# Attention values and sums as matmuls of 64 columns: two banks for a pair of heads, each emptied by one instruction

## The chip, the core and the metric

The kernel runs on one core of a Trainium2 chip. Its engines run side by side: PE multiplies matrices into the banks of PSUM, DVE and ACT work element by element and are the two that empty banks, POOL works element by element on the rest of the memory, and SP issues the transfers. The metric is the device time of one execution in microseconds; lower is better. A "pass" below is one matmul record of the trace on PE: a float32 matmul leaves two records, each with its own load of weights, a float32r matmul leaves one.

## What is computed

```python
scores = scale * q @ k.T                    # 2 batches, 12 heads, 448 tokens, head size 64
scores = cap * tanh(scores / cap)
attn   = exp(scores - max); attn = attn / (sum(attn) + 1e-9)
x      = attn @ v                           # heads side by side: 896 tokens x 768
x      = moe(rms_norm(x) * g)               # gate and value 768 -> 1536, silu, 1536 -> 768
out    = ((x @ w1) * (x @ w2)) @ w3 @ w_out # 768 -> 1024 -> 1024 -> 768
```

Only the step `attn @ v` with its division by the sums is touched.

## The kernel before, in words

The heads are taken in 12 pairs. Scores lie transposed, 128 keys on the partitions by 448 queries, so a head of 448 keys has three chunks of 128 and one of 64. The last chunks of the two heads of a pair share one chunk, `c == 3`: head 0 in partitions 0 to 63, head 1 in 64 to 127. Two pairs are worked off in seven groups `g` of two banks; the fourth group holds the shared chunks of both pairs.

For each group PE makes the scores (`scores`, L430): six float32r matmuls over 64 rows each, which go in twos over the upper and the lower half of the array, or six over 128 rows for the fourth group. ACT takes them out with tanh (L438) and applies exp (L444). Then `pv` (L461) multiplies by the values. Before the change the stationary operand of a chunk is 128 columns wide, 64 of values and 64 of ones, so that one float32 matmul gives a head's values in partitions 0 to 63 of its bank and its sums in 64 to 127. A pair has two banks (tag `o`, two buffers), one for each head, started by its first chunk and stopped by its last; even pairs end with the shared chunk, odd pairs begin with it. Four instructions empty the two banks: `take_sum` twice (ACT L472 or DVE L474) and `take` twice (ACT L182 or DVE L184), 64 partitions each. The sums are inverted on DVE (L489), the values multiplied by them, and squares are summed for the norm. The next pair can only begin when both banks are empty.

Between these steps PE has other work that fills its waits: the first half of a product of the two last weight matrices (`item`, L640 to L642, 64 items of three matmuls over 384 columns), whose weights DVE, ACT and POOL prepare at the same time. Behind all of it, from L807 on, come the experts' products.

The order is not written by hand. A planner (`Plan`) is given every task with its engines and their costs, its rank and the buffers that it holds, plays the engines through by these costs and issues the tasks in the order in which they started there. Each engine then works its instructions off in that order. A grid below is the part of the array that a matmul takes: rows by columns, 128x128, 64x128, and in the changed kernel 128x64 and 64x64.

Of the kernel before, what the change touches and what calls it, by code (L numbers as in the profile page):

```python
# [10 lines left out]
F32 = mybir.dt.float32  # L11
# [3 lines left out]
AF = mybir.ActivationFunctionType  # L15
ALU = mybir.AluOpType
# [3 lines left out]
P = 128  # L20
B, H, S, D = 2, 12, 448, 64
BH = B * H
# [7 lines left out]
NK = 4  # L30
# [136 lines left out]
def body(ctx: ExitStack, tc, qk, v, cap, wgv, wdn, rg, w12, w3t, wo2, out):  # L167
    nc = tc.nc
# [43 lines left out]
    def layer(es, bounded):  # L212
# [12 lines left out]
        def ring(pool, tag, shape, dtype=F32, name=None):  # L225
            return pool.tile(shape, dtype, tag=tag, name=name or tag, bufs=rings[tag])
# [131 lines left out]
        def attend():  # L358
# [52 lines left out]
            def load_val(p):  # L411
                def run(e):
                    vals[p] = ring(ap, "v", [P, 7, P])
                    e.dma_start(out=vals[p], in_=v[p])

                v_done[p] = add(("SP", 0.45), run, first_of(p) - 5.5 if p else -6.85, makes=[vb[p]], size=P * 7 * P * 4)

# [30 lines left out]
            def pv(g, j):  # L448

                use = parts(g)  # L450
                p, c = use[j % len(use)]

                def run(e):
                    start = p % 2 == 0 and c == 0 or p % 2 == 1 and c == 3
                    stop = p % 2 == 0 and c == 3 or p % 2 == 1 and c == 2
                    for i in range(2):
                        rows = slice(i * D, (i + 1) * D) if c == 3 else slice(0, P)
                        if start:
                            pos[2 * p + i] = ring(ps, "o", [P, 512], name="po")
# [5 lines left out]
            def take_sum(i):  # L465
                def run(e):
                    pr, j = divmod(i, 2)
                    if j == 0:
                        sums[pr] = ring(ap, "sm", [P, S])
# [8 lines left out]
            def take(i):  # L478
                def run(e):
                    pr, j = divmod(i, 2)  # L480
                    b, h = divmod(pr, H // 2)
                    half(x_tile(b, h)[j * D : (j + 1) * D], pos[i][:D, :S], e)

                return run
# [39 lines left out]
            for g in range(NG):  # L524
# [12 lines left out]
                for j in range(len(use)):  # L537
# [12 lines left out]
                    r = g + 1.5  # L550
                    done = []
                    for i in range(2):
                        done.append(add(dict(ACT=0.66, DVE=0.66), take_sum(2 * p + i), r - 2 + i * 0.01, after=[a] + done[:1],
                                        makes=[] if i else [smb[p]], uses=[both[i]] + ([smb[p]] if i else [])))
                        new = b not in x_alloc
                        x = add(dict(ACT=0.57, DVE=0.66), take(2 * p + i), r - 2 + 0.1 + i * 0.01, after=[a] + ([] if new else [x_alloc[b]]),
                                makes=[xb[b]] if new else [], uses=[both[i]] + ([] if new else [xb[b]]))
                        x_alloc.setdefault(b, x)
                        done.append(x)
                    inv = [add(("DVE", 1.52), invert(p, c), r + 0.1 * c, after=done, uses=[smb[p]]) for c in range(2)]  # L560
# [101 lines left out]
        def attend_any():  # L662
# [4 lines left out]
            for i in range(BH):  # L667
# [3 lines left out]
                nc.sync.dma_start(out=t, in_=qk[pr])  # L671
                tv = pool.tile([P, 7, P], F32, tag="v", name="tv")
                nc.sync.dma_start(out=tv, in_=v[pr])
# [28 lines left out]
                for k in range(NK):  # L702
                    nc.tensor.matmul(po, tv[:, order[k], :D], pt[:, k, :], start=(k == 0), stop=(k == NK - 1))
                x = x_tile(b, h)
# [418 lines left out]
def _layout(a):  # L1123
# [6 lines left out]
    qk = np.concatenate([q, np.concatenate([one, two], axis=1)], axis=2)  # L1130
    v = np.concatenate([a["v"].reshape(BH, S, D), np.ones((BH, S, D), np.float32)], axis=2).reshape(BH // 2, 2, S, P)
    both = np.concatenate([v[:, 0, 3 * P :], v[:, 1, :D]], axis=1)[:, None]
    v = np.stack([v[:, 0, : 3 * P].reshape(-1, 3, P, P), v[:, 1, D:].reshape(-1, 3, P, P)], axis=2).reshape(-1, 6, P, P)
    v = np.concatenate([v, both], axis=1).transpose(0, 2, 1, 3)
# [31 lines left out]
```

## Time and profile before

| | |
|---|---|
| median of 3 runs | 636.42 us (636.06 to 638.11) |
| the profiled execution | 638.36 us, its span 636.6 us |
| PE busy | 619.9 us (97%) |
| DVE, ACT, POOL busy | 427.2, 284.4, 158.0 us |
| granted clock of PE, mean | 0.995 |

The span is the time from the first to the last instruction of the trace; 1.76 us of the profiled execution lie around it. PE's busy time is no measure of how full it is, since matmuls are pipelined and a record also counts the time in which it waits for the one ahead of it. The distance between the starts of neighbouring records tells more, and is used below.

### The profile page before, as it was taken

Reading aid. Unit: us, or ns where it says so; the run is one execution under the profiler, and the core shown is the slowest. Engines: PE = TensorE matmul, PEld = TensorE weight load, DVE = VectorE, ACT = ScalarE, POOL = GpSimd, SP = SyncE. Lnnn points to the kernel's source line nnn. Section 1 sums busy time; section 2 is a strip of 40 time slices with the busy share of each in tenths; the row PEclk is TensorE's granted clock in tenths of the full one; section 3 lists DMA queues with packets and bytes.
Section 4 is the critical chain, followed back from the end, with each engine's and each line's share of the span. In section 5 each row is a group of like instructions: output and inputs, shape, how many; then the busy total and the mean of one; then the engine's idle time right before and its main releaser. Section 6 shows DMA issues by size and latency. Waiting matters only on the chain.

```text
span 636.6 us, 7787 instructions
## 1 busy us (share of the span) xinstructions
PE 619.9 (97%) x2949; PEld 522.0 (82%) x2949; DVE 427.2 (67%) x543; ACT 284.4 (45%) x392; POOL 158.0 (25%) x153
## 2 busy tenths in 40 slices
PE   6999999999999999999999999999999999999996
PEld 2455556669999999999999999999999999999995
DVE  2898999979867677534777555566656765636743
ACT  6798788965533333322234222344323343313220
POOL 1747532213122344411132222211122121000000
PEclk9899999999999999999999999999999999999998
DMA  8554542325445346224993333323222324105111
GB/s 310 175 198 141 196 142 69 126 74 186 139 146 160 131 133 230 92 67 159 295 315 101 103 118 124 102 100 99 100 99 100 111 89 133 33 1 148 44 59 63
DMA packets 29758, 82.91 MB, mean 130 GB/s; under 512 B 2960, under 2 KB 16912, under 8 KB 29712
## 3 DMA queue, kind: packets, MB, share of 16 engines
q1 hardware_dynamic: 29712, 82.33, 38.9%
q8 instruction: 25, 0.41, 0.3%
q14 instruction: 21, 0.17, 0.1%
HBM read 73.27 MB, written 9.04 MB: 129 GB/s over the span
## 4 chain that ended last, share of the span: by engine, by line
PE 84%; DVE 7%; ACT 5%; issue 2%; POOL 1%; DMA 1%; SPq 0%; DVEq 0%; POOLq 0%
PE bank L808 22%; PE bank L809 22%; PE bank L807 22%; PE bank L1031 8%; PE po L461 4%; ACT t L438 2%; DVE sm L489 2%; PE pss L430 2%; ACT t L444 2%; PE bank L640 1%; PE bank L641 1%; PE bank L642 1%; DVE wraw L270 1%; DVE wraw L274 1%; POOL xraw L497 1%
## 5 line engine op out<-in xcount | busy, mean ns | idle before, releaser
L189 DVE TENSOR_TENSOR whl<-wraw,whl 128x768 fp32r<-128x768 f32 (+1 forms) x86 | 75.7, 882 | 70.4 <-POOL whl L186 58.2
L266 POOL TENSOR_SCALAR wraw<-wraw 128x768 int32<-128x768 uint32 (+1 forms) x67 | 76.1, 1135 | 170.8 <-DMA wraw<-in_w 57.8
L809 PE MATMUL bank<-xn,whl 128*128 128x448 f32 x288 | 106.0, 368 | 0.0
L808 PE MATMUL bank<-xn,whl 128*128 128x448 f32 x288 | 106.0, 368 | 0.0
L807 PE MATMUL bank<-xn,whl 128*128 128x448 f32 x288 | 106.0, 368 | 0.0
L270 DVE SCALAR_TENSOR_TENSOR wraw<-wraw 128x768 int32<-128x768 int32 (+1 forms) x76 | 71.4, 939 | 40.8 <-POOL wraw L266 33.6
L461 PE MATMUL po<-t,v 128*128 128x448 f32 (+1 forms) x192 | 75.5, 565 | 2.8 <-DVE xraw L184 1.2
L274 DVE SCALAR_TENSOR_TENSOR wraw<-wraw 128x768 int32<-128x768 int32 (+1 forms) x76 | 76.8, 1011 | 1.5
L186 POOL TENSOR_SCALAR whl<-wraw 128x768 fp32r<-128x768 f32 (+1 forms) x38 | 34.0, 895 | 166.8 <-PE bank L809 125.2
L809 PE MATMUL bank<-y,whl 128*128 128x448 f32 x192 | 70.7, 368 | 0.0
L807 PE MATMUL bank<-y,whl 128*128 128x448 f32 x192 | 70.7, 368 | 0.0
L808 PE MATMUL bank<-y,whl 128*128 128x448 f32 x192 | 70.7, 368 | 0.0
L182 ACT ACTIVATE whl<-wraw 128x768 fp32r<-128x768 f32 (+1 forms) x48 | 38.1, 795 | 70.6 <-PE bank L809 31.5
L257 ACT ACTIVATE wraw<-wraw 128x768 f32<-128x768 f32 (+1 forms) x55 | 48.5, 882 | 39.4 <-DMA wraw<-in_wgv 14.3
L461 PEld LDWEIGHTS po<-t,v 128*128 128x128 f32 (+1 forms) x192 | 31.5, 192 | 33.8 <-issue 25.9
L808 PEld LDWEIGHTS bank<-xn,whl 128*128 128x128 f32 x288 | 54.1, 188 | 5.5
L807 PEld LDWEIGHTS bank<-xn,whl 128*128 128x128 f32 x288 | 54.1, 188 | 5.4
L809 PEld LDWEIGHTS bank<-xn,whl 128*128 128x128 f32 x288 | 54.1, 188 | 5.4
L809 PE MATMUL bank<-u,whl 128*128 128x448 f32 x144 | 53.0, 368 | 0.0
L807 PE MATMUL bank<-u,whl 128*128 128x448 f32 x144 | 53.0, 368 | 0.0
L808 PE MATMUL bank<-u,whl 128*128 128x448 f32 x144 | 53.0, 368 | 0.0
L438 ACT ACTIVATE t<-pss,small 128x896 f32<-128x896 f32 x42 | 41.9, 998 | 10.3 <-PE pss L430 8.5
(103 smaller groups left out, 1007.5 us busy)
## 6 DMA issues: line engine op xcount, KB each, us to landing
wraw<-in_wgv SPq DMA_DIRECT2D x24, 768.0 KB, 4.4
wraw<-in_w SPq DMA_DIRECT2D x16, 768.0 KB, 4.2
wraw<-in_wdn SPq DMA_DIRECT2D x12, 768.0 KB, 4.2
wraw<-in_w3t SPq DMA_DIRECT2D x16, 512.0 KB, 4.0
wraw<-in_wo SPq DMA_DIRECT2D x8, 768.0 KB, 6.5
v<-in_v SPq DMA_DIRECT2D x12, 448.0 KB, 4.0
qk<-in_qk SPq DMA_DIRECT2D x11, 480.0 KB, 4.1
m_half<-mo SPq DMA_DIRECT2D x16, 192.0 KB, 1.9
```

The lines of the kernel that those rows point to most:

```text
L182: nc.scalar.activation(out_, in_, AF.Copy)
L189: e.tensor_tensor(lo, raw, r32(hi), op=ALU.subtract)
L257: e.activation(h, h, AF.Copy, scale=2.0**-112)
L266: e.tensor_scalar(l, l.bitcast(U32), 0.876 * 2.0**-29, 0.49, op0=ALU.mult, op1=ALU.add)
L270: e.scalar_tensor_tensor(l, h, 3, l, op0=ALU.logical_shift_left, op1=ALU.bitwise_or)
L274: e.scalar_tensor_tensor(l, h, -(2**31), l, op0=ALU.bitwise_and, op1=ALU.bitwise_or)
L438: e.activation(chunks[g], s[:, :, :S], AF.Tanh, scale=tsc)
L461: e.matmul(pos[2 * p + i][:, :S], vals[p][rows, 6 if c == 3 else 2 * c + i, :], x, start=start, stop=stop)
L807: e.matmul(dst, whi[:, c, :], src(0, g, b), start=(g == 0), stop=False)
L808: e.matmul(dst, whi[:, c, :], src(1, g, b), start=False, stop=False)
L809: e.matmul(dst, wlo[:, c, :], src(0, g, b), start=False, stop=(g == total - 1))
L1031: e.matmul(st["bank", name], w[:, q, :], z_at(op, q, y), start=q == 0 and n == 0, stop=q == NQ - 1 and n == 2)
```

## The change

The values lose their columns of ones: `v` is loaded as 7 x 64 columns instead of 7 x 128, and the ones come from the constant tile `ones`. A pair's two banks are divided otherwise: `po` holds the values of both heads, head 0 in partitions 0 to 63 and head 1 in 64 to 127, and `pn` their sums in the same places. Each chunk now takes four float32 matmuls over 64 columns instead of two over 128: values of head 0 and head 1, which take the left and the right half of the array's columns, then sums of head 0 and head 1. For the shared chunk each of them takes 64 rows by 64 columns. One `take_sum` and one `take` over 128 partitions empty the two banks.

```diff
@@ load_val
-                    vals[p] = ring(ap, "v", [P, 7, P])
+                    vals[p] = ring(ap, "v", [P, 7, D])
@@ pv
-                    for i in range(2):
-                        rows = slice(i * D, (i + 1) * D) if c == 3 else slice(0, P)
-                        if start:
-                            pos[2 * p + i] = ring(ps, "o", [P, 512], name="po")
-                        x = chunks[g][rows, j if c == 3 else i, :]
-                        e.matmul(pos[2 * p + i][:, :S], vals[p][rows, 6 if c == 3 else 2 * c + i, :], x, start=start, stop=stop)
+                    if start:
+                        pos[p] = [ring(ps, "o", [P, 512], name=name) for name in ("po", "pn")]
+                    for n in range(2):
+                        for i in range(2):
+                            to = slice(i * D, (i + 1) * D)
+                            rows = to if c == 3 else slice(0, P)
+                            x = chunks[g][rows, j if c == 3 else i, :]
+                            w = ones[rows, :D] if n else vals[p][rows, 6 if c == 3 else 2 * c + i, :]
+                            e.matmul(pos[p][n][to, :S], w, x, start=start, stop=stop)
@@ take_sum, take
-                    s = slice(j * D, (j + 1) * D)
                     if e is nc.scalar:
-                        e.activation(sums[pr][s], pos[i][D:, :S], AF.Identity, bias=guard[D:])
+                        e.activation(sums[pr], pos[pr][1][:, :S], AF.Identity, bias=guard)
                     else:
-                        e.tensor_scalar(sums[pr][s], pos[i][D:, :S], guard[D:], None, op0=ALU.add)
+                        e.tensor_scalar(sums[pr], pos[pr][1][:, :S], guard, None, op0=ALU.add)
...
-                    half(x_tile(b, h)[j * D : (j + 1) * D], pos[i][:D, :S], e)
+                    half(x_tile(*divmod(pr, H // 2)), pos[pr][0][:, :S], e)
@@ the planner's tasks
-                        ("PE", 1.65 if c < 3 else 0.97), pv(g, j), g + 1 + 0.1 * j, after=[exps[g], v_done[p], pv_last.get(p)],
+                        ("PE", 1.65), pv(g, j), g + 1 + 0.1 * j, after=[exps[g], v_done[p], pv_last.get(p)],
...
-                    for i in range(2):
-                        done.append(add(dict(ACT=0.66, DVE=0.66), take_sum(2 * p + i), r - 2 + i * 0.01, after=[a] + done[:1],
...
-                        x = add(dict(ACT=0.57, DVE=0.66), take(2 * p + i), r - 2 + 0.1 + i * 0.01, after=[a] + ([] if new else [x_alloc[b]]),
...
+                    done = [add(dict(ACT=0.55, DVE=0.64), take_sum(p), r - 2, after=[a], makes=[smb[p]], uses=[both[1]])]
+                    done.append(add(dict(ACT=0.55, DVE=0.64), take(p), r - 1.9, after=[a] + ([] if new else [x_alloc[b]]),
```

The planner makes another order of the new tasks. The first place is PE, from the last chunk of the third pair (the shared chunk) to the first chunks of the fourth; the names are `pss` the scores' banks, `t` the exp'd scores, `bank<-wo,whl` the filling items. Before:

```order
L461 MATMUL po<-t,v 128x448 x2
L430 MATMUL pss<-th 128x448 x6
L640 MATMUL bank<-wo,whl 128x384
L641 MATMUL bank<-wo,whl 128x384
L642 MATMUL bank<-wo,whl 128x384
L430 MATMUL pss<-th 128x448 x6
L640 MATMUL bank<-wo,whl 128x384
L641 MATMUL bank<-wo,whl 128x384
L642 MATMUL bank<-wo,whl 128x384
...
L461 MATMUL po<-t,v 128x448 x6
```

The same place of the changed kernel:

```order
L464 MATMUL po<-t,v 64x448 x2
L464 MATMUL pn<-t,ones 64x448 x2
L430 MATMUL pss<-th 128x448 x12
L634 MATMUL bank<-wo,whl 128x384
L635 MATMUL bank<-wo,whl 128x384
L636 MATMUL bank<-wo,whl 128x384
L464 MATMUL po<-t,v 64x448 x2
L464 MATMUL pn<-t,ones 64x448 x2
L464 MATMUL po<-t,v 64x448 x2
L464 MATMUL pn<-t,ones 64x448 x2
```

Between the end of one pair and the start of the next there stood two groups of scores and three filling items, and now there stand two groups and one item. Over the whole stage 33 of the 64 items stood ahead of the last `pv`, and now 15 do. Counted in program order up to the first expert matmul, neighbouring matmuls differ in their grid 61 times before and 78 times now; 12 of the 78 are between 64x128 and 128x128, and 36 lead into a grid of 64 columns.

The second place is DVE, from the emptying of the third pair's banks to that of the fourth pair's (`sm` the sums, `xraw` the values). Before:

```order
L184 COPY xraw<-po 64x448
L474 TENSOR_SCALAR sm<-po,small 64x448
L489 RECIPROCAL sm<-sm 128x224 x2
L189 TENSOR_TENSOR th<-qk,th 128x960
L270 SCALAR_TENSOR_TENSOR wraw<-wraw 128x768
L515 TENSOR_TENSOR acc<-acc,sq 128x448
L474 TENSOR_SCALAR sm<-po,small 64x448
L184 COPY xraw<-po 64x448
L474 TENSOR_SCALAR sm<-po,small 64x448
L489 RECIPROCAL sm<-sm 128x224 x2
```

The changed kernel:

```order
L474 TENSOR_SCALAR sm<-pn,small 128x448
L184 COPY xraw<-po 128x448
L487 RECIPROCAL sm<-sm 128x224 x2
L189 TENSOR_TENSOR th<-qk,th 128x960
L189 TENSOR_TENSOR wo<-wraw,wo 128x768 x2
L513 TENSOR_TENSOR acc<-acc,sq 128x448
L474 TENSOR_SCALAR sm<-pn,small 128x448
L487 RECIPROCAL sm<-sm 128x224 x2
```

Of the 48 instructions that emptied banks DVE had 22 and ACT 26; of the 24 now, DVE has 13 and ACT 11.

## Rows read from the trace of the kernel before

**Rows 1.** Busy time by stretch: length, PE, PEld, DVE, ACT, POOL, clock, DMA share, GB/s.

```profile
60.70:83.00 22.30, 21.02 (x92) 11.84 (x90) 22.10 (x23) 18.10 (x23) 13.40 (x13) 1.00 0.49 157
...
158.20:625.00 466.80, 466.80 (x2292) 427.06 (x2291) 291.67 (x390) 158.56 (x238) 95.83 (x89) 1.00 0.37 121
```

**Rows 2.** PE's groups, 0 to 158 us: count | busy us, mean ns | idle, releasers.

```profile
L461 PE MATMUL po<-t,v 128*128 128x448 f32 x144 | 61.7, 565 | 1.7 <-ACT t L444 0.8 <-ACT xraw L182 0.6 <-DVE xraw L184 0.4
L430 PE MATMUL pss<-th 64*128 64x448 f32 x198 | 29.9, 408 | 1.2 <-ACT t L438 1.2
L640 PE MATMUL bank<-wo,whl 128*128 128x384 f32 x64 | 23.6, 369 | 0.4 <-DVE mo L184 0.4
...
L461 PE MATMUL po<-t,v 64*128 64x448 f32 x48 | 14.2, 567 | 1.1 <-DVE xraw L184 0.8 <-ACT xraw L182 0.3
L430 PE MATMUL pss<-th 128*128 128x448 f32 x33 | 8.8, 400 | 0.0
L430 PE MATMUL pss<-qk 64*128 64x448 f32 x12 | 4.3, 873 | 5.0 <-DMA qk<-in_qk 5.0
L305 PE MATMUL bank<-acc,ones 128*128 128x448 f32 x4 | 1.8, 537 | 0.0
```

**Rows 3.** PE in order of time (start, length): first matmul, an item, first expert.

```profile
5.01 4.28 PE L430 MATMUL pss<-qk 64*128 64x448 f32 x12 [5.01 <-DMA qk<-in_qk]
...
157.21 0.33 PE L640 MATMUL bank<-wo,whl 128*128 128x384 f32 x1
...
158.25 0.36 PE L807 MATMUL bank<-xn,whl 128*128 128x448 f32 x1
```

**Rows 4.** PE in order of time, changes of grid, 37 to 42 us.

```profile
37.10 0.87 PE L430 MATMUL pss<-th 64*128 64x448 f32 x6
37.90 1.77 PE L461 MATMUL po<-t,v 128*128 128x448 f32 x4
39.60 0.86 PE L430 MATMUL pss<-th 64*128 64x448 f32 x6
40.30 0.91 PE L461 MATMUL po<-t,v 64*128 64x448 f32 x4
...
41.74 0.45 PE L640 MATMUL bank<-wo,whl 128*128 128x384 f32 x1
```

**Rows 5.** PE's weight loads in order of time; five neighbours, first and last.

```profile
46.35 0.19 PEld L461 LDWEIGHTS po<-t,v 128*128 128x128 f32 x1 [0.19 <-issue]
...
47.85 0.19 PEld L461 LDWEIGHTS po<-t,v 128*128 128x128 f32 x1 [0.18 <-issue]
```

**Rows 6.** PE in order of time where a pair waits for its banks, 20 to 34 us.

```profile
20.35 1.02 PE L461 MATMUL po<-t,v 64*128 64x448 f32 x2 [0.81 <-DVE xraw L184]
21.64 5.87 PE L461 MATMUL po<-t,v 64*128 64x448 f32 x10 [0.27 <-ACT xraw L182]
27.44 1.50 PE L430 MATMUL pss<-th 64*128 64x448 f32 x12
28.87 1.77 PE L461 MATMUL po<-t,v 128*128 128x448 f32 x4
...
32.01 1.02 PE L461 MATMUL po<-t,v 128*128 128x448 f32 x2 [0.58 <-ACT xraw L182]
33.41 1.02 PE L461 MATMUL po<-t,v 128*128 128x448 f32 x2 [0.37 <-DVE xraw L184]
```

**Rows 7.** Busy time and granted clock (third last column) behind such a wait.

```profile
22.20:25.65 3.45, 3.45 (x6) 1.51 (x5) 3.45 (x3) 3.29 (x4) 0.66 (x1) 0.51 0.31 108
```

**Rows 8.** Groups of instructions that empty the pairs' banks, 0 to 158 us.

```profile
L472 ACT ACTIVATE sm<-po,small 64x448 f32<-64x448 f32 x13 | 8.2, 631 | 0.8 <-PE po L461 0.4
L182 ACT ACTIVATE xraw<-po 64x448 f32<-64x448 f32 x13 | 7.0, 537 | 2.6 <-DVE sm L474 2.4
...
L184 DVE COPY xraw<-po 64x448 f32<-64x448 f32 x11 | 6.8, 616 | 2.3 <-ACT sm L472 2.1
```

**Rows 9.** The page's transfers: KB each, microseconds to landing.

```profile
v<-in_v SPq DMA_DIRECT2D x12, 448.0 KB, 4.0
```

More of the change, by code (lines that the diff above doesn't have):

```diff
@@ L412, in run @@
                 def run(e):
-                    vals[p] = ring(ap, "v", [P, 7, P])
+                    vals[p] = ring(ap, "v", [P, 7, D])
                     e.dma_start(out=vals[p], in_=v[p])
-                v_done[p] = add(("SP", 0.45), run, first_of(p) - 5.5 if p else -6.85, makes=[vb[p]], size=P * 7 * P * 4)
+                v_done[p] = add(("SP", 0.45), run, first_of(p) - 5.5 if p else -6.85, makes=[vb[p]], size=P * 7 * D * 4)
             def scores(g):
@@ L455, in run, with take_sum, take @@
                     stop = p % 2 == 0 and c == 3 or p % 2 == 1 and c == 2
[L456 to L461 removed]
+                    if start:
[7 more added lines that the diff above has]
+                            e.matmul(pos[p][n][to, :S], w, x, start=start, stop=stop)
                 return run
[L465 removed]
+            def take_sum(pr):
                 def run(e):
[L467 to L470 removed]
+                    sums[pr] = ring(ap, "sm", [P, S])
                     if e is nc.scalar:
[L472 removed]
+                        e.activation(sums[pr], pos[pr][1][:, :S], AF.Identity, bias=guard)
                     else:
[L474 removed]
+                        e.tensor_scalar(sums[pr], pos[pr][1][:, :S], guard, None, op0=ALU.add)
                 return run
[L478 removed]
+            def take(pr):
                 def run(e):
[L480 to L482 removed]
+                    half(x_tile(*divmod(pr, H // 2)), pos[pr][0][:, :S], e)
                 return run
@@ L550, in attend @@
                     r = g + 1.5
-                    done = []
-                    for i in range(2):
-                        done.append(add(dict(ACT=0.66, DVE=0.66), take_sum(2 * p + i), r - 2 + i * 0.01, after=[a] + done[:1],
-                                        makes=[] if i else [smb[p]], uses=[both[i]] + ([smb[p]] if i else [])))
-                        new = b not in x_alloc
-                        x = add(dict(ACT=0.57, DVE=0.66), take(2 * p + i), r - 2 + 0.1 + i * 0.01, after=[a] + ([] if new else [x_alloc[b]]),
-                                makes=[xb[b]] if new else [], uses=[both[i]] + ([] if new else [xb[b]]))
-                        x_alloc.setdefault(b, x)
-                        done.append(x)
+                    new = b not in x_alloc
+                    done = [add(dict(ACT=0.55, DVE=0.64), take_sum(p), r - 2, after=[a], makes=[smb[p]], uses=[both[1]])]
+                    done.append(add(dict(ACT=0.55, DVE=0.64), take(p), r - 1.9, after=[a] + ([] if new else [x_alloc[b]]),
+                                    makes=[xb[b]] if new else [], uses=[both[0]] + ([] if new else [xb[b]])))
+                    x_alloc.setdefault(b, done[1])
                     inv = [add(("DVE", 1.52), invert(p, c), r + 0.1 * c, after=done, uses=[smb[p]]) for c in range(2)]
@@ L671, in attend_any @@
                 nc.sync.dma_start(out=t, in_=qk[pr])
[L672 removed]
+                tv = pool.tile([P, 7, D], F32, tag="v", name="tv")
                 nc.sync.dma_start(out=tv, in_=v[pr])
@@ L702, in attend_any @@
                 for k in range(NK):
-                    nc.tensor.matmul(po, tv[:, order[k], :D], pt[:, k, :], start=(k == 0), stop=(k == NK - 1))
+                    nc.tensor.matmul(po, tv[:, order[k], :], pt[:, k, :], start=(k == 0), stop=(k == NK - 1))
                 x = x_tile(b, h)
@@ L1130, in _layout @@
     qk = np.concatenate([q, np.concatenate([one, two], axis=1)], axis=2)
-    v = np.concatenate([a["v"].reshape(BH, S, D), np.ones((BH, S, D), np.float32)], axis=2).reshape(BH // 2, 2, S, P)
+    v = a["v"].reshape(BH // 2, 2, S, D)
     both = np.concatenate([v[:, 0, 3 * P :], v[:, 1, :D]], axis=1)[:, None]
-    v = np.stack([v[:, 0, : 3 * P].reshape(-1, 3, P, P), v[:, 1, D:].reshape(-1, 3, P, P)], axis=2).reshape(-1, 6, P, P)
+    v = np.stack([v[:, 0, : 3 * P].reshape(-1, 3, P, D), v[:, 1, D:].reshape(-1, 3, P, D)], axis=2).reshape(-1, 6, P, D)
     v = np.concatenate([v, both], axis=1).transpose(0, 2, 1, 3)
```

## The prediction

> **What bounds the kernel now.** I read the busy time by stretch first, then PE's groups, then PE in order of time. From 158 us to 625 us PE is busy for the whole stretch at full clock [rows 1]: behind the first expert matmul it waits for nothing, so what the change does ahead of that point moves the end by as much. Ahead of it DVE is nearly as full as PE in places (22.10 of 22.30 us, [rows 1]), and the question is which of the two sets the pace.
>
> So I draw up an account of PE from its first matmul, 5.01 us, to the first expert matmul, 158.25 us [rows 3]: 153.2 us. The price of each kind of work is the distance between starts where PE runs without a break:
>
> - A float32 pass over 448 columns: from the first to the last of five weight loads 1.50 us [rows 5], so 0.375. The 144 passes over 128x128 [rows 2] take 54.0.
> - The 48 passes over 64 rows [rows 2] go in twos: four of them start at 40.30, six passes of scores follow, and the item behind these starts 1.44 us later [rows 4]. That is two slots of 0.375, the scores and little more. So 24 slots, 9.0.
> - Six passes of scores over 64 rows: twelve take 1.43 (27.44 to 28.87, [rows 6]), six 0.80 (37.10 to 37.90, [rows 4]); the difference, 0.63, is the work of six. 198 of them [rows 2] are 33 times 0.63, 20.8. The 33 over 128 rows at a third of that, 0.21 each, are 6.9.
> - A filling item: two take 1.04 (157.21 to 158.25, [rows 3]), so 64 items [rows 2] take 33.3.
> - The first pair's scores, 12 float32 passes in twos, 2.3, and four passes of `L305`, 1.5 [rows 2].
>
> Together 127.8. What is over from the six passes, 0.80 - 0.63 = 0.17, and from `pv` between scores, 37.90 to 39.60 = 1.70 less four passes, 0.20 [rows 4], is what PE loses when the grid changes: part of it before the change (the matmuls ahead run out), part behind it (a load of weights that nothing covers). The scores at 39.60 have only the part behind, since the shared chunk that follows has their grid: 0.70 - 0.63 = 0.07 [rows 4]. I take 0.19 for one change; 61 of them are 11.6. The rest, 153.2 - 139.4 = 13.8 us, are waits and slow clock. So PE's work with its grid changes is 91% of the stage, and DVE's load, however full, can only show in the 13.8.
>
> Of these, the waits for the pairs' banks are seen best at 20 to 34 us. At 20.35 the second pair's first `pv` has waited 0.81 us for DVE's copy, and its other half for ACT's until 21.64 [rows 6]. From 20.35 to 27.44 PE does four half passes (two slots) and eight full ones, 3.75, and one change and a half of grid, 0.3; it takes 7.09. The other 3.0 are the halves going one after the other, the second wait, and the clock: behind the gap the granted clock is 0.51 of full speed for 3.45 us [rows 7], which is the lower level, 1.2 GHz. At 32.01 and 33.41 the third pair waits again, 0.58 us and then some 0.6 between the two starts that are not work [rows 6]. That makes 0.8 + 3.0 + 0.6 + 0.6 = 5.0 us behind banks that four instructions empty, two on each bank, 0.54 to 0.63 us apiece [rows 8].
>
> **The change part by part.**
>
> *PE, chunks of 128 keys.* 72 matmuls over 128 columns become 144 over 64. If left and right half of the columns run side by side, as upper and lower half of the rows do [rows 4], a chunk takes four slots as before: nothing.
>
> *PE, the shared chunk.* Two matmuls, two slots side by side, become four, four slots: values and sums no longer come out of one matmul, and there is no other half of the array to give the sums to. 12 chunks x 2 slots x 0.375 = **+9.0 us**. Nothing hides it, since PE sets the pace.
>
> *PE, changes of grid.* 78 for 61: `pv` shares its grid with nothing now, neither with the filling items nor, for the shared chunk, with the scores. 17 x 0.19 = **+3.2 us**. No row shows a grid of 64 columns. From below, the part behind the change could vanish with the shorter load of weights; from above it is the 0.19 of any other change. The part behind the change is about half of it (0.07 of 0.17 above), and I estimate that half as many columns take half as long to load: 36 entries x 0.04 = **-1.4 us**; the ends are -3.4 (36 x 0.095) and 0.
>
> The Trainium skill (TensorE: Matmul & The Clock Gate, LDWEIGHTS) gives a load as columns over 1.2 GHz, so 53 ns less for 64 columns than for 128. By that the 36 entries would give back an estimated 1.9 us in place of 1.4; no run here shows it yet.
>
> *Emptying the banks.* 24 instructions for 48, over 128 partitions for 64. Nothing shows one over 128 partitions out of these banks; I take the 0.54 to 0.63 us of the old ones [rows 8], since they have as many elements in each partition. From above, at twice that, nothing is won. One instruction on each of ACT and DVE empties both banks at once, and the order has two groups of scores and an item to cover it, 2 x 0.63 + 0.52 and two changes, some 2.1 us. I let the whole 5.0 go: **-5.0 us**; the ends are 0, and with the other waits that the freed 14 us of ACT and DVE could shorten, some -10 (3 of the 13.8 are the start, where the first scores wait for ACT and run at low clock).
>
> *Order and transfers.* 18 items move behind the last `pv`: they are paid there instead, at the same price, and give DVE longer to finish the second batch's norm before the experts need it: nothing. The values' transfers halve, from 448 KB in 4.0 us [rows 9]; the scores, tanh and exp that lie ahead of a `pv` hide them, and none of PE's groups names them as a releaser [rows 2]: nothing; uncovered, 4.0 us for the first.
>
> Sum: 9.0 + 3.2 - 1.4 - 5.0 = **+5.8 us**. The profiled execution took 638.36 us (span 636.6 and 1.76 around it), so 644.2 against it; the median of the three runs is 1.9 lower, and against that I forecast **642.2 us**. With all waits kept it is +10.8, 647.2; with the best ends (-3.4 and -10) -1.2, 635.2.
>
> **The rivals.**
>
> *The waits vanish altogether, no change.* Those of 20 to 34 us are not the only ones: a DVE freed of 9 instructions and an ACT freed of 15 could give up the others. For it: DVE is 99% busy in one stretch [rows 1]. Against: the freed time matters only at the gaps. 9.0 + 3.2 - 1.4 - 10 = +0.8, 637.2.
>
> *The shared chunk's halves do not run together.* Before, they wrote to two banks; now both write to one, in different partitions and from different rows. If one waits for the other, each of the 12 chunks takes eight slots in place of four: 12 x 4 x 0.375 = +18, 660.2. No row shows two halves of the rows at work in one bank. The Trainium skill (TensorEngine Tiling, Gotcha 1: PSUM Pressure) says that different row tiles cannot access the same PSUM bank at once; by that this rival is the forecast. I hold it down because the two meet in no partition.
>
> *Halves of the columns do not run together.* Both read all 128 partitions, while the halves of rows that the trace shows read their own. If they go one after the other, each of 36 chunks takes eight slots: 36 x 1.5 = +54, and the shared ones +18 as well; the remaining waits, some 8, would drown in it: 642.2 + 72 - 8, about 706. For it: nothing in the trace has two matmuls reading the same partitions. Against: a float32r pass takes 0.21 us for the same columns [rows 4, 6], so a float32 pass asks for little more than half of what the array can be fed.
>
> *Changes to and from a grid of 64 columns are free, faster.* Then only the 12 between 64x128 and 128x128 are paid, 2.3 for 11.6: 9.0 - 9.3 - 5.0 = -5.3, 631.1. It decides if a change with such a grid costs under about 0.08 us (9.0 + 2.3 + 66 x price = 11.6 + 5.0). For it: no such grid was seen. Against: both directions between the grids that are seen cost about the same [rows 4].
>
> **How the numbers follow.** Forecast with its own range of 638.5 to 647.2: 0.62. Waits vanish: 0.13. Shared halves apart: 0.08. Column halves apart: 0.08. Free changes: 0.09. A measurement of this kernel can tell 0.3%, 1.9 us, from no change: faster is below 634.5, slower above 638.3. Faster: free changes and a sliver of the vanished waits, 0.10. Same: the rest of these, 0.13. Slower: 0.77. The range leaves out free changes and column halves apart, 0.17: from 636 to 661.
>
> **What would show it.** Starts of `pv` passes in twos a few ns apart with 0.375 us between twos say that column halves run together; four slots for the shared chunk, that its halves do. Scores between two `pv` at 0.80 and a lone `pv` at 1.65 to 1.70 say that the changes of grid are priced rightly. No gap at the second pair's start and a granted clock of 1.00 behind 20 us say that the 5.0 were won. The account up to the first expert matmul should come to about 159 us, with eight to nine of waits in it, and PE should be busy throughout behind it. The forecast is wrong if the waits only move: if with 15 items in place of 33 PE runs out of filling work and stands in front of tanh or exp, or if the experts find their weights late.

## The result and the profile after

The changed kernel takes 641.78 us (641.05 to 643.49); the kernel before, on the same chip, 637.46 us (635.54 to 640.34). The ratio is 1.0067, with an interval of 1.0048 to 1.0086: 4.3 us slower, where 5.8 were forecast. The profiled execution took 643.46 us, span 641.7.

Busy time by stretch of the changed kernel, with the columns of [rows 1] and the stretch of [rows 7]; PE's groups up to the first expert matmul, with the columns of [rows 2], follow it:

```profile
20.00:80.00 60.00, 56.31 (x310) 23.88 (x310) 59.43 (x57) 49.18 (x58) 33.77 (x31) 1.00 0.50 159
22.20:25.65 3.45, 3.45 (x22) 1.11 (x16) 3.45 (x3) 1.93 (x3) 2.35 (x3) 1.00 0.40 140
60.70:83.00 22.30, 22.30 (x129) 9.89 (x129) 21.76 (x27) 19.18 (x23) 8.57 (x10) 1.00 0.46 141
165.03:625.00 459.97, 459.97 (x2270) 423.24 (x2270) 287.71 (x383) 158.67 (x239) 97.93 (x92) 1.00 0.37 124
```

The first of these stretches in the kernel before, and below it the one group of [rows 2] that waited there and is not among them:

```profile
20.00:80.00 60.00, 57.14 (x228) 31.01 (x230) 57.39 (x56) 50.68 (x60) 34.96 (x31) 0.97 0.53 176
```

```profile
L641 PE MATMUL bank<-wo,whl 128*128 128x384 f32 x64 | 21.6, 338 | 1.3 <-DVE wo L189 1.3
```

PE's groups of the changed kernel:

```profile
L464 PE MATMUL po<-t,v 128*64 128x448 f32 x144 | 34.4, 556 | 0.6 <-DVE sm L474 0.5
L464 PE MATMUL pn<-t,ones 128*64 128x448 f32 x144 | 33.2, 539 | 0.0
L430 PE MATMUL pss<-th 64*128 64x448 f32 x198 | 28.0, 392 | 0.4 <-ACT t L438 0.4
L634 PE MATMUL bank<-wo,whl 128*128 128x384 f32 x64 | 22.7, 354 | 2.8 <-ACT mo L182 2.7
...
L464 PE MATMUL po<-t,v 64*64 64x448 f32 x48 | 11.6, 562 | 2.8 <-DVE xraw L184 1.5 <-DVE sm L474 1.3
L464 PE MATMUL pn<-t,ones 64*64 64x448 f32 x48 | 11.0, 536 | 0.0
...
L430 PE MATMUL pss<-qk 128*128 128x448 f32 x2 | 1.0, 591 | 0.3 <-ACT t L438 0.3
```

The granted clock is 1.00 where [rows 7] had 0.51, and the 12 transfers of the values land in 3.5 us for the 4.0 of [rows 9]. Behind the first expert matmul PE is busy throughout, as before. In front of it the waits have other places: behind the emptying of the banks 3.3 us (1.5, 1.3 and 0.5), where [rows 6] has 2.0, and at the filling items 2.8, nearly all behind ACT's `mo` copies, where the kernel before had 1.7 (0.4 and 1.3). PE in order of time (start, length) shows these, and the slots:

```profile
16.80 0.86 PE L430 MATMUL pss<-th 64*128 64x448 f32 x6
17.59 0.97 PE L464 MATMUL po<-t,v 64*64 64x448 f32 x4
18.39 0.92 PE L464 MATMUL pn<-t,ones 64*64 64x448 f32 x4
19.24 0.87 PE L430 MATMUL pss<-th 64*128 64x448 f32 x6
21.62 0.97 PE L464 MATMUL po<-t,v 64*64 64x448 f32 x4 [1.51 <-DVE xraw L184]
...
32.66 0.97 PE L464 MATMUL po<-t,v 128*64 128x448 f32 x4 [0.55 <-DVE sm L474]
...
36.62 0.97 PE L464 MATMUL po<-t,v 128*64 128x448 f32 x4
37.42 0.92 PE L464 MATMUL pn<-t,ones 128*64 128x448 f32 x4
38.27 0.86 PE L430 MATMUL pss<-th 64*128 64x448 f32 x6
39.06 0.97 PE L464 MATMUL po<-t,v 64*64 64x448 f32 x4
...
43.21 0.33 PE L636 MATMUL bank<-wo,whl 128*128 128x384 f32 x1
44.82 0.97 PE L464 MATMUL po<-t,v 64*64 64x448 f32 x4 [1.27 <-DVE sm L474]
...
149.45 0.34 PE L636 MATMUL bank<-wo,whl 128*128 128x384 f32 x1
152.48 0.41 PE L634 MATMUL bank<-wo,whl 128*128 128x384 f32 x1 [2.69 <-ACT mo L182]
...
165.03 0.36 PE L801 MATMUL bank<-xn,whl 128*128 128x448 f32 x1
```

A slot is the 0.375 us of one float32 pass, or of two that run side by side. Four passes into `po` take two slots: from 36.62 to 37.42 it is 0.80 us, two slots and the entry into the new grid. So left and right columns run side by side, and in the shared chunk (17.59 to 19.24) the two diagonal quarters do, though they write one bank. The shared chunk has four slots where [rows 4] had two.

The stage from the first matmul (5.10) to the first expert (165.03) is 159.94 us long for 153.24 before: +6.7. By the prices of the prediction its work is now 136.8 us (54.0, 18.0 for the shared chunks, 20.8, 6.9, 33.3, 2.3, 1.5). For the grid changes the row at 36.62 gives `pv` 1.65 us up to the scores and these 0.79, where [rows 4] has 1.70 and 0.80: one cycle is 0.06 us shorter. So 78 x 0.19 less 36 x 0.06 make 12.7. That leaves 10.4 us of waits and slow clock for 13.8. In short: +9.0 slots, +1.1 grid changes, -3.4 waits and slow clock. This is bookkeeping at fixed prices and does not say what a slot would give back; the experiments ask that.

The -3.4 is not idle time of PE, which rose: behind the first matmul the groups show 6.9 us now (0.6, 0.4, 2.8, 2.8 and 0.3) and 5.7 before (1.7, 1.2, 0.4, 1.1 of [rows 2] and 1.3 of `L641`). What fell is time in which PE worked more slowly than by its prices. The half clock of [rows 7] is a part of it, an estimated 1.7 us (half of 3.45); the changed kernel's profile has no such stretch in the stage (e8's, with the same instructions up to the first expert, has one, from 151.5). The rest was not taken apart.

Behind the first expert the changed kernel takes 476.64 us for 478.31, though it has the same matmuls there: the last of them ends 2.5 us sooner, counted from the first, and what follows it takes 0.8 longer. The 2.5 were not expected; e7 asks where they come from, and e8 to e12 take account of it.

### The profile page after: what moved, and what is told of

Same layout as the page of the kernel before. It is cut to its first block, busy times and chain, and to the rows that moved or that the text cites. A ratio compares the mean times of both kernels' runs of the same rounds, so it can differ in the third digit from the quotient of the medians.

```text
span 641.7 us, 8149 instructions
## 1 busy us (share of the span) xinstructions
PE 623.0 (97%) x3141; PEld 513.8 (80%) x3141; DVE 421.2 (66%) x532; ACT 279.7 (44%) x384; POOL 154.3 (24%) x148
## 4 chain that ended last, share of the span: by engine, by line
PE 89%; DVE 3%; DMA 3%; ACT 2%; POOL 1%; SPq 0%; issue 0%; DVEq 0%; ACTq 0%; POOLq 0%
PE bank L803 22%; PE bank L801 22%; PE bank L802 22%; PE bank L1025 8%; PE po L464 5%; PE pn L464 4%; PE pss L430 4%; DMA wraw<-in_wgv 1%; PE bank L634 1%; DMA wraw<-in_wo 1%; PE bank L636 1%; PE bank L635 1%; DVE sm L487 1%; DVE wraw L274 1%; DVE wraw L270 0%
## 5 line engine op out<-in xcount | busy, mean ns | idle before, releaser
L186 POOL TENSOR_SCALAR whl<-wraw 128x768 fp32r<-128x768 f32 (+1 forms) x35 | 32.2, 919 | 171.4 <-PE bank L803 124.1
L182 ACT ACTIVATE whl<-wraw 128x768 fp32r<-128x768 f32 (+1 forms) x51 | 40.7, 800 | 70.9 <-PE bank L803 30.4
L257 ACT ACTIVATE wraw<-wraw 128x768 f32<-128x768 f32 (+1 forms) x57 | 49.8, 874 | 45.5 <-DMA wraw<-in_wgv 15.0
L464 PE MATMUL po<-t,v 128*64 128x448 f32 (+1 forms) x192 | 46.0, 557 | 3.4 <-DVE sm L474 1.8
L444 ACT ACTIVATE t<-t,small 128x896 f32<-128x896 f32 x42 | 43.8, 1043 | 1.3
```

The costliest lines, as they stand in the source:

```text
L257: e.activation(h, h, AF.Copy, scale=2.0**-112)
L444: e.activation(chunks[g], chunks[g], AF.Exp, scale=acap)
L464: e.matmul(pos[p][n][to, :S], w, x, start=start, stop=stop)
```

## The experiments

The stage is read from each kernel's one profile; the times are medians, and each ratio is to runs of the kernel before beside them (medians 637.05 to 638.23). One profile's stage is good to no better than 1 to 2 us: three pairs of kernels have the same instructions up to the first expert, and their stages are 153.24 and 155.12 (before and e7), 159.94 and 160.81 (changed and e8), 153.78 and 155.38 (e2 and e9).

| kernel | us | ratio to before, interval | stage, us |
|---|---|---|---|
| changed | 641.78 | 1.0067 (1.0048 to 1.0086) | 159.94 |
| e1 no shared sums | 638.94 | 1.0016 (0.9994 to 1.0038) | 157.41 |
| e2 four tiles | 638.91 | 1.0022 (1.0005 to 1.0039) | 153.78 |
| e3 split emptying | 646.81 | 1.0137 (1.0108 to 1.0167) | 163.40 |
| e4 before, shared twice | 643.43 | 1.0097 (1.0066 to 1.0128) | 158.64 |
| e5 four tiles, kept order | 643.64 | 1.0098 (1.007 to 1.0126) | 159.87 |
| e6 first weights on GpSimd | 646.18 | 1.0134 (1.0103 to 1.0166) | 160.28 |
| e7 before, short matmuls | 630.91 | 0.9891 (0.987 to 0.9913) | 155.12 |
| e8 changed, short matmuls | 636.11 | 0.9979 (0.9959 to 1.0) | 160.81 |
| e9 e2, short matmuls | 631.69 | 0.99 (0.9869 to 0.9931) | 155.38 |
| e10 e5, short matmuls, busy wait | 635.69 | 0.9967 (0.9947 to 0.9987) | 158.57 |
| e11 e9, busy waits | 630.54 | 0.9893 (0.9863 to 0.9924) | 153.53 |
| e12 e10, half reciprocals | 631.13 | 0.9897 (0.9872 to 0.9923) | 153.19 |

### What the shared chunk's slots cost: e1, e2, e4

e1 leaves out the shared chunks' matmuls for the sums:

```diff
-                    for n in range(2):
+                    for n in range(1 if c == 3 else 2):
...
```

> The changed kernel in its own order, with the sums of the shared chunk left out (24 matmuls; the sums then lack its 64 keys). Theory: these 24 slots of 0.375 us stand on PE, which sets the pace, so 9.0 us go: 632.8 us, 4.7 below the kernel before. Rival: ACT's tanh and exp set the pace of the stage and PE would only wait longer; then it stays at 640 to 642.

e2 crosses the sums of the two heads in their bank, so that the shared chunk's four matmuls stand on four different quarters; the sums are then emptied by two instructions that cross them back, and the order is planned with 0.97 us for this `pv`:

```diff
-                            to = slice(i * D, (i + 1) * D)
-                            rows = to if c == 3 else slice(0, P)
+                            to = slice((i ^ n) * D, ((i ^ n) + 1) * D)
+                            rows = slice(i * D, (i + 1) * D) if c == 3 else slice(0, P)
...
```

> The changed kernel, with the sums of a pair crossed in their bank (head 0 in partitions 64 to 127, head 1 in 0 to 63), so that the shared chunk's values and sums take the four different quarters of the array; the sums are then emptied by two instructions of 64 partitions in place of one. Theory: the cost is that values and sums of the shared chunk go one after the other; four quarters at work together take two slots in place of four, 9.0 us less, and the 12 more instructions on ACT or DVE cost 0 to 1 us: 633 to 634 us, below the kernel before. Rival: quarters that share rows, or that write with others into one bank, wait for each other: 641 to 643.

e4 is the kernel before with the shared chunk's two matmuls issued twice, which doubles that chunk's part of the output:

```diff
+                    for again in range(2 if c == 3 else 1):
...
```

> The kernel before in its own order, the shared chunk's matmuls issued twice (its keys then count double). Theory: 24 more slots of 0.375 us are paid in full also in the old order, 9.0 us more: 646.5 us. Rival: the 13.5 us of waits in the stage before the experts take part of them in: 639 to 643.

Taking the 24 slots away gave back 2.8 us (e1) and 2.9 us (e2); adding as many to the kernel before cost 6.0. None is the full 9.0, and each of the three times lies between its theory and its rival. In the profiled stage alone the differences are 2.5, 6.2 and 5.4 us: the medians also hold what happens behind the first expert, where e1 and e4 are faster than e2 (see e7). In e2 the slots are gone, as PE in order of time shows:

```profile
17.33 0.59 PE L464 MATMUL po<-t,v 64*64 64x448 f32 x2
17.34 0.59 PE L464 MATMUL pn<-t,ones 64*64 64x448 f32 x2
...
18.24 0.87 PE L430 MATMUL pss<-th 64*128 64x448 f32 x6
...
38.54 0.87 PE L430 MATMUL pss<-th 64*128 64x448 f32 x6
41.23 0.88 PE L430 MATMUL pss<-th 64*128 64x448 f32 x6 [1.82 <-ACT t L438]
...
42.83 0.52 PE L638 MATMUL bank<-wo,whl 128*128 128x384 f32 x1
44.55 0.69 PE L639 MATMUL bank<-wo,whl 128*128 128x384 f32 x1 [1.20 <-DVE whl L189]
```

The chunk takes 0.91 us up to the scores, where the changed kernel took 1.65. But PE, ahead of time now, stands 1.82 us in front of a `tanh` and 1.20 in front of a weight, and from 42.1 to 49.0 the granted clock is 0.5, the lower level. e1 is alike: 1.83 us in front of a `tanh` and 1.23 behind DVE's emptying, and 0.5 from 44.0 to 50.9. In e4 the waits at 20 us are there, but the clock does not fall behind them (1.00 from 19 to 26, for the 0.51 of [rows 7]). So part of a slot's price is paid or given back in waits and in clock.

e2 differs from the changed kernel in more than the slots: its order is planned anew, with 24 of the 64 items ahead of the last `pv` in place of 15, so that its gain is that of slots and order together.

### What the emptying gives: e3

e3 splits each emptying instruction of the changed kernel into two of 64 partitions, in the same order:

```diff
+                    for s in (slice(0, D), slice(D, P)):
...
-                        e.tensor_scalar(sums[pr], pos[pr][1][:, :S], guard, None, op0=ALU.add)
+                            e.tensor_scalar(sums[pr][s], pos[pr][1][s, :S], guard[s], None, op0=ALU.add)
...
```

> The changed kernel in its own order, each emptying instruction of 128 partitions split into two of 64. Theory: the waits fell by about 3.5 us because two instructions empty a pair in place of four; with four again most of that comes back, 644 to 645.5 us. Rival: the waits fell because the order and the clock changed, and half a microsecond more at a pair's end is hidden by the scores behind it: 641.5 to 642.5.

It is 5.0 us slower than the changed kernel (3.5 in the profiled stage), more than this experiment expected. The groups that empty the banks, of the changed kernel and then of e3:

```profile
L474 DVE TENSOR_SCALAR sm<-pn,small 128x448 f32<-128x448 f32 x8 | 5.4, 679 | 11.3 <-PE pn L464 11.3
L182 ACT ACTIVATE xraw<-po 128x448 f32<-128x448 f32 x7 | 3.7, 524 | 0.0
```

```profile
L475 DVE TENSOR_SCALAR sm<-pn,small 64x448 f32<-64x448 f32 x16 | 10.9, 684 | 8.2 <-PE pn L464 8.0
L182 ACT ACTIVATE xraw<-po 64x448 f32<-64x448 f32 x14 | 7.4, 531 | 0.1
```

An instruction over 128 partitions takes as long as one over 64 (679 and 684 ns, 524 and 531 ns): joining two of them halves the time. Some of the 5.0 is clock: e3 has 3.4 us at 0.5 from 46.4, an estimated 1.7 us.

### The slots with the order kept, and the new wait: e5, e6

e5 puts e2's four quarters into the changed kernel's order: one planned step empties the sums with two instructions.

```diff
+                    for i in range(2):
+                        s, o = (slice(j * D, (j + 1) * D) for j in (i, 1 - i))
...
-                        e.tensor_scalar(sums[pr], pos[pr][1][:, :S], guard, None, op0=ALU.add)
+                            e.tensor_scalar(sums[pr][s], pos[pr][1][o, :S], guard[o], None, op0=ALU.add)
```

> The changed kernel, with the order of its instructions kept; only the shared chunk's four matmuls go to the four quarters of the tile array (the sums' two halves are crossed in their bank), so that they take two slots in place of four, and the sums of a pair are emptied by two instructions of 64 partitions, one behind the other on the same engine. Theory (the 24 slots are TensorE time at full price once nothing else in the order moves): -9.0 us for the slots, +1.3 to +2.5 us for the twelve more instructions on ScalarE and VectorE (half of the 24 that the split emptying added at +5.0): 641.8 - 9.0 + 1.3 to 2.5 = 634.1 to 635.3. Rival (the stage ahead of 50 us is set by ScalarE and VectorE, so a shorter TensorE stream only waits longer there, and the granted clock falls to 0.5 behind that wait): 638.5 to 639.5, as the two earlier kernels without the four slots gave, with waits of over 1 us between 39 and 46 us and a stretch at 0.5 right behind them.

Both expectations missed: 643.64, 1.9 us slower than the changed kernel, though PE has 9.0 us less to do. The signs of the rival were there, a wait and the half clock, from 43.9 to 50.7:

```profile
45.32 1.01 PE L464 MATMUL po<-t,v 64*64 64x448 f32 x2 [2.08 <-DVE sm L476]
```

e5 also has twelve more emptying instructions than the changed kernel; by half of e3's 5.0 they cost an estimated 2.5 us.

In the changed kernel, ACT in order of time shows what stands ahead of the `mo` copies:

```profile
146.30 0.48 ACT L182 ACTIVATE mo<-bank 128x384 f32<-128x384 f32 x1
151.06 0.90 ACT L257 ACTIVATE wraw<-wraw 128x768 f32<-128x768 f32 x1 [4.28 <-DMA wraw<-in_wgv]
151.85 0.86 ACT L182 ACTIVATE mo<-bank 128x384 f32<-128x384 f32 x2
```

e6 takes that `L257` off ACT, for the first four expert weights (`alone`):

```diff
-            unary = dict(POOL=0.25 + N / 1000, ACT=0.2 + N / 1200)
+            unary = dict(POOL=0.25 + N / 1000, **({} if alone else dict(ACT=0.2 + N / 1200)))
...
```

> The changed kernel, with the two unary steps and the first rounding of the first four expert weights on GpSimd alone, so that ScalarE's copies of the wo products into mo no longer stand behind a step that waits for an expert weight's transfer (in the changed kernel ScalarE waits 4.3 us for it until 151.06, and TensorE 2.7 us for the copy behind it). TensorE's order in the stage is kept. Theory (that wait costs what it shows): the gap of 3.0 us at 149.4 shrinks to under 1 us, 641.8 - 2.0 to 2.7 = 639.1 to 639.8. Rival (the next thing is late: VectorE's six multiplications hold up the last wo weight until 152.55, or the first expert weights come late from GpSimd): 641 to 643, with a gap of 2 to 3 us at the same place or at the first experts.

Neither range held: 646.18. PE's wait is still there, 2.1 us from 148.7, behind ACT's copy again; and the copy now waits 4.8 us for the transfer that stores an older `mo`. Among the experts PE stalls at 177.3, 1.3 us from one start to the next, for a weight that DVE finishes late, as the rival had it. In both kernels the copies so wait for a transfer, of a weight or of `mo`; what makes these transfers late was not tried.

### The spacing of the experts' matmuls: e7

Matmuls over 448 columns, counted in two stretches behind the first expert (the first number in brackets is the count on PE), in the kernel before, the changed kernel and e7:

```profile
170.00:290.00 120.00, 120.00 (x582) 109.00 (x582) 74.76 (x87) 40.91 (x61) 39.99 (x35) 1.00 0.41 136
340.00:620.00 280.00, 280.00 (x1357) 254.36 (x1356) 167.62 (x236) 92.80 (x142) 43.45 (x41) 1.00 0.28 92
```

```profile
170.00:290.00 120.00, 120.00 (x594) 111.23 (x593) 80.40 (x94) 44.30 (x65) 40.35 (x36) 1.00 0.42 139
340.00:620.00 280.00, 280.00 (x1356) 254.33 (x1356) 170.46 (x239) 92.91 (x141) 43.97 (x42) 1.00 0.29 94
```

```profile
170.00:290.00 120.00, 120.00 (x594) 111.23 (x593) 78.06 (x89) 42.13 (x63) 39.00 (x37) 1.00 0.41 138
340.00:620.00 280.00, 280.00 (x1383) 259.47 (x1382) 170.55 (x241) 93.26 (x143) 43.47 (x41) 1.00 0.28 93
```

The kernel before has 582 in 120 us throughout, 206 ns apart. The changed kernel has 594 there, 202 ns, and the wide spacing again behind the `wo` products, which have another number of columns. In its trace the closer spacing begins where one weight load came 30 ns late, 3.5 us behind the first expert; e1, e3, e4 and e5 too have it up to the `wo` products, e2 and e6 do not. e7 is the kernel before with a short matmul at two such places:

```diff
+                    if g == 0 and (k, b) in ((1, 0), (at + CF2, 1)):
+                        e.matmul(dst[:, :D], whi[:, c, :], src(0, g, b)[:, :D], start=True, stop=True)
```

> The kernel before, with two throw-away matmuls of 64 columns: one ahead of the second item of the first half of the experts, one ahead of the second item of the second half; each writes 64 columns of a bank that the next matmul starts anew. It asks about an observation, not about the change: in the profiles the experts' matmuls over 448 columns are 206.7 ns apart in the kernel before, and on average 202.7 ns apart up to the wo products in those kernels in which a matmul or a weight load came late by itself shortly after the experts began. Theory (the spacing is set by how the stream of weight loads and matmuls stands against itself after such a stumble, and stays until the shape changes): spacing 202.7 behind both places, 645 x 4.0 ns and some 1,400 x 4.0 ns, so 637.4 - 8.0 = 629 to 630 (or 634.8 if only the first place takes it up). Rival (a late semaphore, or another work load in the other engines, sets it, not the stream): 206.7 throughout and 637.4 to 637.7.

At that place in the code `D` is 2, not 64, so the throw-away matmul has two columns, not the 64 of the expectation:

```profile
163.74 0.37 PE L811 MATMUL bank<-xn,whl 128*128 128x448 f32 x1
163.95 0.17 PE L808 MATMUL bank<-xn,whl 128*128 128x2 f32 x1
163.98 0.45 PE L809 MATMUL bank<-xn,whl 128*128 128x448 f32 x1
164.26 0.36 PE L810 MATMUL bank<-xn,whl 128*128 128x448 f32 x1
```

The spacing came out as in the theory, with 594 and 1383 matmuls in the two stretches; the time, 630.91 us, 6.9 faster than before, is 0.9 us above its range. In e7's profile the spacing is 206.7 ns up to each of the two short matmuls and 202.7 on average behind it. A stumble does not always do it: in the same profile PE waits 1.1 us in front of the first expert, the second matmul comes 0.07 us late, and the wide spacing follows all the same. The traces do not tell in what the two spacings differ inside PE.

### The change at one spacing: e8 to e12

e8 is the changed kernel with e7's edit, and e9 is e2 with it.

> The changed kernel with the two throw-away matmuls of 64 columns ahead of expert items, so that the experts' matmuls are 202.7 ns apart in every execution and the change can be compared with the kernel before at one and the same spacing (630.91 us). Theory (the change costs what the stage in front of the experts shows, 159.94 - 153.24 = +6.7, and some executions of both kernels already had the closer spacing in part): the difference of the two at one spacing is +4.5 to +7, so 635.4 to 637.9. Rival (the stage's +6.7 was one execution's, and the +4.3 to +5.8 of the medians held a difference of spacing): under +4, so below 634.9.

> The four-quarters kernel (shared chunk in two slots, sums crossed in their bank, order planned anew) with the same two throw-away matmuls. Theory: the stage as measured (153.8) and the closer spacing (-7.9 behind the experts, whose profile had 206.7 throughout): 638.9 - 7.9 = 631.0, level with the kernel before at that spacing (630.9). Rival (the saved slots do not come back, and more than half of its executions had the closer spacing already): 633 to 636.

At one spacing the change costs 636.11 - 630.91 = 5.2 us; by their ratios to before, 0.9% or 5.6 us. The theory of e8 held. e9 is 4.4 us faster than e8 and 0.8 slower than e7, near its theory (631.0).

e10 is e5 with e7's edit, and PE has throw-away matmuls over unused columns where e5's PE waited from 42.9; e11 is e9 with seven of these between an item's second and third matmul, and ten over 64 columns ahead of the shared `pv` at 37.6. The line for e10:

```diff
+                    if (kb, n, r) == (0, 0, 0):
+                        for _ in range(10):
+                            e.matmul(mb[kb, n][:, NH:], ones, ones, start=False, stop=False)
```

> The changed kernel with the shared chunk on four quarters, its order of instructions kept, the two throw-away matmuls ahead of expert items, and ten throw-away matmuls over 128 unused columns behind TensorE's first wo item, in the place where that order waited 2.4 us (42.9 to 45.3) and then worked at a granted clock of 0.5 for 6.8 us. Theory (of the 9.0 us of slots taken away, that wait and the half clock took 2.4 + 3.4): with TensorE busy through the wait the clock stays at 1.0 and the stage is 3.4 us shorter, 159.9 - 3.4 = 156.5, so 643.6 - 3.4 - 5 (spacing of the second half) = 635 to 636. Rival (the clock falls all the same, or falls later): 638 to 640 and a stretch at 0.5.

> The four-quarters kernel planned anew with the two throw-away matmuls ahead of expert items, and throw-away matmuls in unused columns where its stage waited: ten over 64 columns ahead of the values of the shared chunk at 37.6, seven over 128 columns between the first wo item's second and third matmul at 42.8. Theory: no stretch at 0.5 between 42 and 49, -3.4 us: 627 to 628, faster than both kernels by over 9 us. Rival (the half clock moves to the next wait, or the throw-away work itself delays the emptying): 630 to 632.

The granted clock (third last column) from 39 to 51 us, of e5 and then of e10:

```profile
39.00:51.00 12.00, 8.76 (x41) 3.23 (x35) 11.89 (x11) 7.62 (x9) 7.10 (x6) 0.72 0.22 66
```

```profile
39.00:51.00 12.00, 10.83 (x75) 5.98 (x73) 11.89 (x11) 7.44 (x8) 7.37 (x6) 1.00 0.20 61
```

With work in the wait the clock stays at 1.00; the mean granted clock of whole runs is 0.994 to 0.998 in the twelve of e10, 0.987 to 0.995 in the six of e5. e10's time fell into the range of its theory, but that was reckoned from e5. Against e8, which has the four slots, it wins 0.4 us, with the clock full and 9.0 us less on PE. That is net of the twelve more emptying instructions, an estimated 2.5 us: in that order the slots and the clock together are worth an estimated 3 us, near the 2.8 of e1, and not 9.0. e11 wins 1.2 us on e9, not 3.4, though its clock is full too: 630.54, in its rival's range. The clock did not fall elsewhere, as the rival had it; whether the throw-away work delays the emptying, its other reason, was not looked into.

e12 asks whether the rest is DVE, which is busy 11.89 of 12 us above. It takes each reciprocal of e10 over half its columns (the other half of the sums stays uninverted):

```diff
-                    r = sums[pr][:, c * S // 2 : (c + 1) * S // 2]
+                    r = sums[pr][:, c * S // 2 : (2 * c + 1) * S // 4]
```

> The kernel with the shared chunk on four quarters, the order kept and TensorE busy in its first wait, with each of the 24 reciprocals of the sums taken over 112 of its 224 columns (the other half of the sums is left uninverted, so half of the attention's output is not the reference's). The order on every engine stays. Between 20 and 80 us this takes 12 x about 0.76 = 9 us from VectorE, which was busy 58.5 of those 60 us, and no work from TensorE. Theory (the slots taken from TensorE did not come back there because VectorE's work, 99% of the time from 35 to 80 us, sets the pace, and the emptying by two instructions adds to it): 635.7 - 4 to 6 = 629.5 to 631.5, with the waits of the stage gone in part. Rival (the waits are of ScalarE, GpSimd and of an order made for a longer TensorE stream, whatever VectorE does): 634.5 to 635.7.

631.13 us, in the range of its theory and 4.6 less than e10, with the same work and order on PE. Busy time by stretch, of e10 and then of e12:

```profile
35.00:80.00 45.00, 43.51 (x262) 19.98 (x258) 44.63 (x45) 34.75 (x42) 23.64 (x22) 1.00 0.44 146
80.00:95.00 15.00, 13.10 (x77) 5.71 (x76) 12.13 (x15) 11.96 (x15) 2.85 (x2) 1.00 0.22 65
```

```profile
35.00:80.00 45.00, 44.69 (x277) 20.79 (x274) 43.32 (x49) 38.08 (x44) 25.10 (x22) 1.00 0.47 158
80.00:95.00 15.00, 14.73 (x78) 7.84 (x76) 8.89 (x12) 12.62 (x16) 4.96 (x3) 1.00 0.07 18
```

PE gets through 277 matmuls in place of 262, and its idle time from 80 to 95 us goes from 1.90 to 0.27. So in e10 the pace up to 80 us is DVE's. For the changed kernel this is argued from the same order and from its 59.43 of 60 us; halving its own reciprocals was not tried.

## Why the prediction was right, step by step

- **Halves side by side.** Right, for columns and for the shared chunk's diagonal quarters; both rivals that had them apart (706 and 660.2) fall. The Trainium skill (TensorEngine Tiling, Gotcha 1: PSUM Pressure) would have kept the two row halves from writing one bank together; the trace disagrees where they write different partitions of it: four passes in 0.80 us at 17.59.
- **The shared chunk, +9.0.** The slots are there. "Nothing hides it, since PE sets the pace" is the step that was too strong. Added to the kernel before, these slots cost 6.0 (e4); taken from the changed kernel, with an order made for it, 4.4 (e8 to e9) to 5.6 (e8 to e11, clock included); with the order kept, 2.8 (e1, with the waits and the half clock that came in their place) or 0.4 (e8 to e10, net of twelve more emptying instructions). The account of PE, 91% of the stage, did not see that from 20 to 80 us DVE is as near its limit: 59.43 of 60 us in the changed kernel, 57.39 before. e12 showed for e10's kernel that DVE sets the pace there.
- **Grid changes, +1.8.** Mechanism right, some +1.1: an entry into 64 columns saves 0.06 us, not 0.04. The Trainium skill (TensorE: Matmul & The Clock Gate, LDWEIGHTS) gave 0.053; the cycle of 1.65 + 0.79 us bears it out within its rounding. That such changes are free (631.1) falls: the scores alone still take 0.79.
- **Emptying, -5.0.** Too large. That joining the instructions pays is shown, since undoing it costs 5.0 (e3); that this is the same number is chance, for the 5.0 of the prediction were the waits from 20 to 34 us, and these did not all go. "No gap at the second pair's start" did not come true: 1.51 us are left there, since one instruction is still waited for, 0.55 at 32.66, and 1.27 at 44.82 are new. Together PE stands 3.3 us behind banks, for 2.0 in [rows 6] (0.81, 0.27, 0.58, 0.37). What went is the half clock behind 20 us and the halves that ran one after the other. The clock of 1.00 there came true, and the mean granted clock of whole runs fits it: 0.996 to 0.999, median 0.998, in the ten of the changed kernel, and 0.993 to 0.999, median 0.996, in the 23 of the kernel before beside e1 to e4. Yet e4 kept 1.00 there with the waits of the kernel before (0.77 and 0.27 us), so a shorter wait is not shown to be the reason. All waits and slow clock together fell by 3.4.
- **Order, nothing.** Too low. PE waits 2.8 us at the items, at 149.4 for ACT's `mo` copies, for 1.7 at the items before; e6 did not remove it. The 1.27 at 44.82 stand where one item fills the time in place of three, and filling work that runs out was among the prediction's signs of being wrong; that this is their cause is argued, since the changed kernel with as many items between its pairs as before was not tried.
- **The sum.** 9.0 + 1.1 - 3.4 = 6.7 in the profiled stage, less 1.7 behind it (2.5 by the closer spacing, 0.8 more at the end): 5.0, the difference of the two spans (641.7 and 636.6) within 0.1. At one spacing e7 and e8 measure 5.2 for the 5.8 forecast. That the terms add up so well is in part luck: the slots at full price were too much, the emptying of -5.0 too much the other way, and the 2.5 of the closer spacing were in no term.

The waits' rival (637.2) was the nearest: it asked whether a freed DVE buys more, and e12 says that DVE is what to free. But the waits that were left and the new ones kept the change from getting there.

## What to carry to other kernels

Before a matmul is put in or left out, see which engine is full in that stretch: PE's account of 91% and a DVE busy for 59 of 60 us can both be true. Here 9 us of PE time were then worth 4.4 to 6.0 us, and 2.8 in an order made for the longer work (e1). Joining two instructions over 64 partitions into one over 128 halved their time here (679 ns for twice 684), and splitting them again cost 5.0 us. Where a long even stream of matmuls runs, count how many fit into a stretch in several kernels: here a difference there was worth 6.9 us, more than the change itself.

## What was not expected of the hardware

- The same float32r matmuls over 448 columns run 206 or 202 ns apart for hundreds of microseconds, at the same granted clock of 1.00. A short stumble (30 ns late, or a matmul of two columns) was followed by the closer spacing, which held until the number of columns changed. A stall of 1.3 us in e6, and one of 1.1 us in front of e7's first expert, left the wide spacing as it was. Two short matmuls make the kernel before 6.9 us faster (e7, 630.91), as fast as the best version of the change (e11, 630.54).
- Four matmuls on four quarters of 64x64, into two banks, run together: four starts within 20 ns, eight passes and the change to the scores' grid in 0.91 us (e2).
- The granted clock of 0.5 at e5's wait did not come with throw-away matmuls in that wait (0.72 for e5, 1.00 for e10 from 39 to 51 us). Clock and slots together gained little there, 0.4 us net, and e12 shows that DVE set the pace.
